# One attention and feed-forward kernel: sign tiles cleared on VectorE, block additions as separate plan entries, later landing times in the planner, casts on ScalarE, and the seven-product first layer from unit 3 on

## The chip, the cores and the metric

The kernel runs on one core of one Trainium2 chip. The metric is the device time of one launch in microseconds (us). Engines are called PE (TensorE), DVE (VectorE), ACT (ScalarE), POOL (GpSimd) and SP (SyncE, which here only issues transfers).

## The reference

Windowed attention with 8 global and 96 local keys and a slope per head, followed by a two-layer feed-forward block with a leaky activation:

```
scores = q @ k.T / sqrt(64) - slope[h] * dist          # B=4, H=8, S=768, D=64, masked to the window
a      = exp(scores - max) / (sum + 1e-9)
x      = (a @ v) as 3072 tokens x 512
h      = x @ w_in                                      # 512 x 2048
g      = max(h, 0) + alpha * min(h, 0)
out    = g @ w_out                                     # 2048 x 512, float32
```

## The kernel before

The 3072 tokens are cut into 12 units (u = 0 to 11) of 256 tokens. For each unit and each of 8 heads, `attend` makes the scores on PE (tile `sp`), the row minimum with bias on DVE (L651, `pr`, `sm`), the exponential on ACT (L656), a high and a low float16 part of the probabilities (`ps`), a transposing transfer on SP (`vp`), and the product with v on PE (`av`). `xn` is the normalised result of a unit.

Then the feed-forward block. All float32 operands are split in a high part (a cast, ACT or DVE) and a low part (the remainder, DVE, helper `rest`, L363 or L364), and every product is three float16 matmuls: high*high, high*low, low*high. The weights come as float64; `split_w` rebuilds a float32 from its two words (16 blocks f, tiles `wf`, `whl`). For blocks f from 6 on it uses two sign tiles `sg0`, `sg1` that `clear_signs` sets to zero once, on POOL.

The first layer has two forms. For u below `US` = 4, `ff_in2` computes `h` plainly: 16 blocks of 12 matmuls of 256 columns each (L894), `g` with one ACT scaling and one DVE step (L903), and its two halves `gg`. For u from 4 on, `ff_in4` computes four blocks f at once by a seven-product scheme on 2 x 2 blocks: 4 times 7 products of 12 matmuls of 128 columns in a unit (L827, banks `hx`, `hy`, `hz`), with sums of weight blocks `sw` (`combine_w`, eight of them, from `ws`) and sums of token blocks `t12`, `t34` (`x_combine`) in place of some operands, and with joins (L838, L855) and the activation (L863) on DVE in the tile `hs`, split as `ghl`. `ff_out` is the second layer, the same in both forms: 16 x 2 x 3 matmuls of 512 columns in a unit (L925).

The order of all work is made in the kernel itself. Every step is entered with a key (its due place), an engine and a cost (`op`, `copy`, `mul`, `rest`); `Plan.order` runs a list of events with these costs, with delays between engines (`LAG`), with the number of buffers of each tag, and picks on each engine the ready entry with the lowest key. Some entries have two possible engines: a first and another that takes it when the first has a long queue (`behind`, `FLEX`). The instructions are then issued in that order; each engine works strictly in order. A new cost or delay therefore moves many instructions by a few places. In the planner an SP entry is a transfer that is taken to land `LAG["SP"]` after its transfer time.

Of the kernel before, what the change touches and what calls it, by code (L numbers as in the profile page):

```python
# [136 lines left out]
class Plan:  # L137
# [7 lines left out]
    LAG = {"PE": 220, "DVE": 130, "ACT": 200, "POOL": 160, "SP": 1100}  # L145
# [27 lines left out]
    def order(self):  # L173
# [34 lines left out]
        while events:  # L208
# [11 lines left out]
            for e in engines:  # L220
# [73 lines left out]
LEAD1 = 22  # L294
# [10 lines left out]
XENG = ('DVE', 'DVE', 'POOL', 'ACT')  # L305
# [4 lines left out]
US = 4  # L310
QU = 4
SIGN = 6
# [12 lines left out]
def fast(tc, cn, a):  # L325
    nc = tc.nc
    ctx = ExitStack()
    with ctx:
# [184 lines left out]
        def combine_w(j, key):  # L513
# [4 lines left out]
            for i, x in enumerate((one_, two_)):  # L518
                cols = slice(512 * i, 512 * i + 512)
                on = lambda e, x=x, cols=cols: e.tensor_tensor(  # L520
                    out=r.t[:, cols], in0=x.t[:, 0, :512], in1=x.t[:, 1, :512], op=ALU.add)
                op("DVE", key, c_dve(512), lambda on=on: on(v), r=[(x, 0), (x, 2)], w=[(r, i)])

            def combine():
                q = [r.t[:, 256 * i : 256 * i + 256] for i in range(4)]
                v.tensor_tensor(out=q[3], in0=q[2], in1=q[3], op=ALU.add)
                v.tensor_tensor(out=q[2], in0=q[0], in1=q[2], op=ALU.subtract)
                v.tensor_tensor(out=q[0], in0=q[3], in1=q[0], op=ALU.subtract)
                v.tensor_tensor(out=q[1], in0=q[1], in1=q[0], op=ALU.subtract)
# [49 lines left out]
        def attend(u, h, key):  # L579
# [10 lines left out]
            if u > 1 and h % 2 == 0:  # L590
# [572 lines left out]
```

## Time and profile before

| what | value |
|---|---|
| median of 3 runs | 608.58 us (606.15 to 612.18) |
| the profiled execution | 606.35 us, its span 604.6 us |
| granted TensorE clock, mean | 0.996 of 2.4 GHz |
| busy: PE, DVE, ACT, POOL | 586.3, 502.8, 420.8, 3.9 us |
| first and last plain product (`h`) of units 2 and 3 | 140.4 to 185.7 us, 185.7 to 236 us |
| last matmul of the second layer | 595.9 us |

A busy PE means that matmuls are in flight; matmuls overlap, so that the price of one is read from the distance of the starts. The same holds for DVE, where a row's duration runs some 0.07 us into the next row's.

### The profile page before, as it was taken

To read this page: it belongs to the slowest core of one execution; us is meant where nothing else is said; L and a number is where in the kernel's file an instruction comes from. 1 tells how busy PE (TensorE), PEld (TensorE's weight loads), DVE (VectorE), ACT (ScalarE), POOL (GpSimd) and SP (SyncE) were. 2 spreads that over 40 slices of the span, in tenths; PEclk is the share of its full clock that TensorE was granted. 3 is DMA by queue.
4 is the path that set the end of the run, shared out by engine and by line. 5 is a ranking of instruction groups with operands and counts; after the bars stand their busy time and mean duration, and the time that the engine had idled before them with its cause. 6 is when DMAs were issued, how large, how long until landed. Compare 5 with 4: busy or idle time off the path is not lost.

```text
span 604.6 us, 15888 instructions
## 1 busy us (share of the span) xinstructions
PE 586.3 (97%) x6215; PEld 414.8 (69%) x6215; DVE 502.8 (83%) x1345; ACT 420.8 (70%) x1109; POOL 3.9 (1%) x13
## 2 busy tenths in 40 slices
PE   7999999999899999999999999999999999999994
PEld 6877666666566666877777777767777777777762
DVE  7999999999899979898799789788798788664441
ACT  5988999897747757778588688677586676552421
POOL 2000000000000000000000000000000000000000
PEclk9999999999999999999999999999999999999998
DMA  8996344355844436556649647539648625312001
GB/s 313 413 382 233 114 116 113 80 116 150 144 93 126 122 97 145 136 113 136 141 94 150 151 94 146 144 77 149 114 110 169 143 63 111 85 37 27 36 1 41
DMA packets 133795, 78.98 MB, mean 131 GB/s; under 512 B 114896, under 2 KB 116688, under 8 KB 133712
## 3 DMA queue, kind: packets, MB, share of 16 engines
q1 hardware_dynamic: 132992, 76.71, 51.6%
q10 hardware_dynamic: 720, 1.18, 0.6%
q8 instruction: 50, 0.82, 0.6%
q14 instruction: 33, 0.27, 0.1%
HBM read 43.79 MB, written 6.29 MB: 83 GB/s over the span
## 4 chain that ended last, share of the span: by engine, by line
PE 78%; DVE 16%; ACT 2%; issue 1%; DMA 1%; DVEq 0%; ACTq 0%
PE o L925 35%; PE hx L827 14%; PE h L894 8%; PE hy L827 7%; PE av L709 4%; PE hz L827 3%; PE sp L628 3%; PE sp L635 2%; DVE pr L651 2%; DVE ws L520 1%; DVE g L903 1%; DVE sw L363 1%; ACT pr L656 1%; DVE ps L364 1%; DVE gg L363 1%
## 5 line engine op out<-in xcount | busy, mean ns | idle before, releaser
L925 PE MATMUL o<-whl,ghl 128*128 128x512 f16 (+1 forms) x771 | 193.8, 379 | 0.0
L827 PEld LDWEIGHTS <-sw 128*128 128x128 f16 x1536 | 93.4, 98 | 21.1 <-issue 0.4
L925 PEld LDWEIGHTS <-ghl 128*128 128x128 f16 x771 | 66.9, 98 | 55.5 <-issue 5.1
L656 ACT ACTIVATE pr<-pr,sm 128x256 f32<-128x256 f32 (+1 forms) x192 | 92.4, 483 | 13.0 <-DVE sm L651 12.9
L894 PE MATMUL h<-xt,whl 128*128 128x256 f16 x768 | 92.3, 273 | 3.5 <-ACT g L344 2.2
L925 PE MATMUL o<-whl,gg 128*128 128x512 f16 x384 | 92.1, 379 | 1.8 <-DVE gg L363 1.7
L894 PEld LDWEIGHTS <-whl 128*128 128x128 f16 x768 | 73.7, 98 | 21.9 <-issue 7.7
L827 PEld LDWEIGHTS <-whl 128*128 128x128 f16 x1152 | 71.0, 98 | 18.9 <-issue 0.2
L651 DVE CUSTOM_DVE_ANT_0 pr<-sp,D 128x256 f32<-128x256 f32 (+1 forms) x192 | 69.8, 395 | 13.1 <-PE sp L628 12.0
L835 ACT ACTIVATE g<-hx 128x256 f32<-128x256 f32 x96 | 36.4, 380 | 60.4 <-PE hx L827 60.2
L863 DVE SCALAR_TENSOR_TENSOR hs<-hs,alpha 128x256 f32<-128x256 f32 x128 | 58.4, 479 | 18.0 <-ACT hs L835 17.1
L925 PEld LDWEIGHTS <-gg 128*128 128x128 f16 x384 | 35.6, 98 | 40.8 <-DVE gg L363 5.8
L364 DVE SCALAR_TENSOR_TENSOR ps<-pr,ps 128x512 f16<-128x512 f32 (+1 forms) x80 | 51.3, 643 | 7.6 <-ACT ps L344 7.4
L363 DVE TENSOR_TENSOR ghl<-hs,ghl 128x512 f16<-128x512 f32 x64 | 42.0, 685 | 2.2 <-ACT ghl L870 2.1
L870 ACT CAST ghl<-hs 128x512 f16<-128x512 f32 x64 | 36.8, 611 | 2.4 <-DVE hs L863 2.4
L344 ACT ACTIVATE ps<-pr 128x512 f16<-128x512 f32 (+1 forms) x60 | 36.1, 601 | 0.9
L656 ACT ACTIVATION_READ_ACCUMULATOR pr<-pr,sm 128x1 f32 x192 | 36.6, 191 | 0.0
L344 ACT ACTIVATE g<-h,ak 128x256 f32<-128x256 f32 x60 | 27.6, 462 | 9.8 <-PE h L894 9.7
L709 PEld LDWEIGHTS <-vp 128*128 128x128 f16 x888 | 30.5, 98 | 3.6
L835 ACT ACTIVATE hs<-hx 128x256 f32<-128x256 f32 x32 | 12.1, 379 | 29.1 <-PE hx L827 29.0
L709 PE MATMUL av<-vp 128*128 128x64 f16 x888 | 32.4, 193 | 0.0
L344 ACT ACTIVATE qs<-qk 128x672 f16<-128x672 f32 (+1 forms) x32 | 23.5, 733 | 12.2 <-PE sp L628 8.5
(137 smaller groups left out, 874.0 us busy)
## 6 DMA issues: line engine op xcount, KB each, us to landing
w<-in_w_dram SPq DMA_DIRECT2D x32, 512.0 KB, 8.3
qk<-in_qk_dram SPq DMA_DIRECT2D x28, 336.0 KB, 3.8
v<-in_vw_dram SPq DMA_DIRECT2D x28, 256.0 KB, 3.6
out_dram<-os SPq DMA_DIRECT2D x19, 256.0 KB, 3.5
qk<-in_qk_dram SPq DMA_DIRECT2D x12, 272.0 KB, 3.1
v<-in_vw_dram SPq DMA_DIRECT2D x12, 192.0 KB, 3.1
first<-in_first_dram SPq DMA_DIRECT2D x4, 464.0 KB, 4.7
first<-in_first_dram SPq DMA_DIRECT2D x4, 336.0 KB, 9.1
```

What stands on the lines that cost most here:

```text
L344: lambda: nc.scalar.mul(out=out(), in_=src(), mul=by.t if tile_ else by)),
L363: return e.tensor_tensor(out=out(), in0=src(), in1=hi(), op=ALU.subtract)
L364: return e.scalar_tensor_tensor(out=out(), in0=src(), scalar=val(), in1=hi(), op0=ALU.mult, op1=ALU.subtract)
L651: op("DVE", key, c_dve(n) + 10, lambda qb=qb, n=n, dc=dc, pc=pc: v.tensor_tensor_reduce(out=pr.t[:, pc : pc + n], in0=sp.t[:, pc : pc + n] ...
L656: op("ACT", key + 1, c_act(n, ptr=1) + 93, lambda qb=qb, n=n, pc=pc: nc.scalar.activation(out=pr.t[:, pc : pc + n], in_=pr.t[:, pc : pc + ...
L709: nc.tensor.matmul(out, lhsT=p_[:, 128 * j : 128 * j + 128], rhs=v_[:, 64 * j : 64 * j + 64], start=m == 0, stop=m == len(ps) - 1)
L827: nc.tensor.matmul(bank.t[:, 128 * q : 128 * q + 128], lhsT=wt(q, wi, c), rhs=xp(xi, c), start=begin and q == n == 0, stop=n == 5, skip_gr ...
L835: op("ACT", k, c_act(UT, True), lambda: nc.scalar.mul(out=out(), in_=two(bank), mul=KG), r=[bank], w=w, spare=SPARE if u < NU - 1 else 0)
L863: op("DVE", ks[4 + 2 * i], c_dve(UT, ptr=True), lambda n=n: v.scalar_tensor_tensor(out=hs.t[:, n, :], in0=hs.t[:, n, :], scalar=alpha[:, 4 ...
L870: op("ACT", ks[6], c_act(512), lambda q=q, cols=cols: nc.scalar.copy(out=ghl.t[:, 0, cols], in_=flat(q)), r=src, w=[(ghl, q)])
L894: nc.tensor.matmul(hp.t[:, cols], lhsT=w.t[:, wi, wc], rhs=x.t[:, NC * xi + c, :], start=n == 0, stop=n == 3 * NC - 1)
L925: nc.tensor.matmul(o.t[:, cols], lhsT=g_()[:, tok], rhs=w.t[:, wi, 512 + cols.start : 512 + cols.stop], start=f == 0 and n == 0, stop=f == ...
```

## The change

- `clear_signs` moves from POOL to DVE and is entered ahead of all other work; the tiles are set as 672 words of 32 bits each.
- The four additions of `combine_w` and of `x_combine`, each one plan entry before, become four entries with their own dependences, and `inverse` becomes `total` and `inverse`. The planner now takes 125 (before 60) between dependent DVE entries (`OWN`).
- Landings: `LAG["SP"]` 1100 becomes 2100, loads of q, k and v get 1500 more (`LOADS`), and a store on ACT's queue holds its buffer 2500 longer (`LANDS`).
- The v cast of units 2 and 3 has ACT as its first engine, as has the cast of the token block of unit 2 (`XENG`).
- `US` 4 becomes 3: unit 3 takes `x_combine` and `ff_in4`. `LEAD1` 22 becomes 24 (attention of unit 1 is due 2 earlier). The output tile of unit 1 uses the tag `pt`.

```diff
-    LAG = {"PE": 220, "DVE": 130, "ACT": 200, "POOL": 160, "SP": 1100}
+    LAG = {"PE": 220, "DVE": 130, "ACT": 200, "POOL": 160, "SP": 2100}
...
-                heapq.heappush(events, (end + self.LAG[e], i, "free"))
+                heapq.heappush(events, (end + self.LAG[e] + LANDS * (self.way[i].__name__ == "on_act"), i, "free"))
...
-                        at[j][x] = max(at[j][x], end + ((0 if e == "PE" else 60) if own else self.LAG[e] + self.spare[i]))
+                        at[j][x] = max(at[j][x], end + (OWN.get(e, 60) if own else self.LAG[e] + self.spare[i]))
...
-LEAD1 = 22
+LEAD1 = 24
...
-XENG = ('DVE', 'DVE', 'POOL', 'ACT')
+XENG = ('ACT', 'DVE', 'POOL', 'ACT')
...
-US = 4
+US = 3
 QU = 4
+LOADS = 1500
+LANDS = 2500
+OWN = {'PE': 0, 'DVE': 125}
...
         def clear_signs(key):
             for i in range(2):
                 x = buf("qs", f"sg{i}", [P, 1344], F16)
-                op("POOL", key, 1500, lambda x=x: nc.gpsimd.memset(x.t, 0.0), w=[x])
+                op("DVE", key, 700, lambda x=x: v.memset(x.t, 0.0), w=[x])
...
-            def combine():
-                q = [r.t[:, 256 * i : 256 * i + 256] for i in range(4)]
-                v.tensor_tensor(out=q[3], in0=q[2], in1=q[3], op=ALU.add)
-                v.tensor_tensor(out=q[2], in0=q[0], in1=q[2], op=ALU.subtract)
-                v.tensor_tensor(out=q[0], in0=q[3], in1=q[0], op=ALU.subtract)
-                v.tensor_tensor(out=q[1], in0=q[1], in1=q[0], op=ALU.subtract)
-
-            op("DVE", key, 4 * c_dve(256), combine, r=[], w=[r])
+            q = lambda i: r.t[:, 256 * i : 256 * i + 256]
+            for to, x, y, how in ((3, 2, 3, ALU.add), (2, 0, 2, ALU.subtract), (0, 3, 0, ALU.subtract), (1, 1, 0, ALU.subtract)):
+                op("DVE", key, c_dve(256), lambda to=to, x=x, y=y, how=how: v.tensor_tensor(
+                    out=q(to), in0=q(x), in1=q(y), op=how), r=[(r, x if y == to else y)] if to in (x, y) else [(r, x), (r, y)], w=[(r, to)])
...
-                    out=x.t[:, : 256 + nk], in_=a["qk"][u - 2, h // 2, :, : 256 + nk]), w=[x])
+                    out=x.t[:, : 256 + nk], in_=a["qk"][u - 2, h // 2, :, : 256 + nk]), w=[x], spare=LOADS)
...
-                mul(kp + 3, lambda: vhi()[:, :nv], vv, XS, [rv], [rvh], "ACT" if u >= US else "DVE", nv)
+                mul(kp + 3, lambda: vhi()[:, :nv], vv, XS, [rv], [rvh], "ACT", nv)
...
-                op("DVE", key + 3, 280, inverse, r=[(sm, (x, 2 + y)) for x in range(G) for y in range(2)], w=[(sm, "inverse")])
+                op("DVE", key + 3, 80, total, r=[(sm, (x, 2 + y)) for x in range(G) for y in range(2)], w=[(sm, "total")])
+                op("DVE", key + 3, 120, inverse, r=[(sm, "total")], w=[(sm, "inverse")])
...
-            op("DVE", key + 0.1, 4 * c_dve(256), combine, r=[x], w=[t12, t34])
+            combine(lambda: half(t12, 0), lambda: q(2), lambda: q(0), [x], [(t12, 0)])
+            combine(lambda: half(t34, 0), lambda: q(3), lambda: q(2), [x], [(t34, 0)])
+            combine(lambda: half(t12, 1), lambda: q(3), lambda: half(t12, 0), [x, (t12, 0)], [(t12, 1)])
+            combine(lambda: half(t34, 1), lambda: q(1), lambda: half(t12, 1), [x, (t12, 1)], [(t34, 1)])
...
-                s = buf("stage", f"os{u}_{t}", [P, 512]) if f == NF - 1 else None
+                s = buf("pt" if u == 1 else "stage", f"os{u}_{t}", [P, 512]) if f == NF - 1 else None
...
-        jobs = [(-99, clear_signs, ()), (-100, build_bias, ()), (-100, warm, ()), (slot(NU - 1, 6), check, ())]
+        jobs = [(-101, clear_signs, ()), (-100, build_bias, ()), (-100, warm, ()), (slot(NU - 1, 6), check, ())]
```

What the planner makes of it at three places. First, the start of the program on DVE (`ones`, `nf`, `tt`, `n2` are small constants, `ni` holds the two window sizes, `far` begins the bias). Before:

```order
L1111 MEMSET ones_63 128x128
L1124 CAST nf_68<-ni_66 128x4
L1126 SCALAR_TENSOR_TENSOR tt_70<-nf_68 128x2
L1127 SCALAR_TENSOR_TENSOR n2_69<-tt_70,nf_68 128x2
L405 TENSOR_SCALAR far_184<-rel_156,n2_69 128x256
```

With the change:

```order
L1115 MEMSET ones_63 128x128
L468 MEMSET sg0_156 128x672
L468 MEMSET sg1_182 128x672
L1128 CAST nf_68<-ni_66 128x4
L1130 SCALAR_TENSOR_TENSOR tt_70<-nf_68 128x2
L1131 SCALAR_TENSOR_TENSOR n2_69<-tt_70,nf_68 128x2
```

The two clears stand ahead of `nf` on DVE; on POOL they stood last, behind the making of `rel` and `gcol`.

Second, DVE in unit 3, where the first half of the activations (`gg3_0` before, `ghl3_0` now) is made for PE. Before:

```order
L903 SCALAR_TENSOR_TENSOR g3_0_2664<-h3_0_2635,g3_0_2664 128x512
L345 TENSOR_SCALAR g3_1_2780<-h3_1_2746,ak_153 128x256
L353 CAST sw6_2735<-ws6_2680 128x512
L364 SCALAR_TENSOR_TENSOR ps4_4_2778<-pr4_4_2719,ps4_4_2778 128x512
L363 TENSOR_TENSOR gg3_0_2783<-g3_0_2664,gg3_0_2783 128x512
```

With the change:

```order
L529 TENSOR_TENSOR ws5_2751<-ws5_2751 128x256
L865 SCALAR_TENSOR_TENSOR hs3_0_2749<-hs3_0_2749,alpha_65 128x256
L529 TENSOR_TENSOR ws5_2751<-ws5_2751 128x256
L865 SCALAR_TENSOR_TENSOR hs3_0_2749<-hs3_0_2749,alpha_65 128x256
L857 TENSOR_TENSOR hs3_0_2749<-g3_0_1_2782 128x2x128
L366 TENSOR_TENSOR sw5_2830<-ws5_2751,sw5_2830 128x512 x2
L650 ISA pr4_6_2927,sm4_4_2689<-sp4_6_2848,D6_216 128x256
L650 ISA sm4_4_2689 128x1
L865 SCALAR_TENSOR_TENSOR hs3_0_2749<-hs3_0_2749,alpha_65 128x256
```

In place of one activation step and one remainder there are joins, four activation steps and two remainders (`ghl3_0`, a few rows on), and the weight sums `ws5`, `sw5`, single entries now, stand between them.

Third, SP around the loads of q and k for unit 4. Before:

```order
L593 DMA qk4_0_2056<-in_qk_dram 128x672
L695 DMA_TRANSPOSE vp3_4_1934<-ps3_4_2092 128x6x128
L593 DMA qk4_2_2152<-in_qk_dram 128x672
L695 DMA_TRANSPOSE vp3_5_1951<-ps3_5_2111 128x6x128
L596 DMA v4_2_2185<-in_vw_dram 128x512
```

With the change:

```order
L592 DMA qk4_0_2086<-in_qk_dram 128x672
L697 DMA_TRANSPOSE vp3_4_1937<-ps3_4_2111 128x6x128
L697 DMA_TRANSPOSE vp3_5_1941<-ps3_5_2152 128x6x128
L592 DMA qk4_2_2185<-in_qk_dram 128x672
L595 DMA v4_2_2194<-in_vw_dram 128x512
```

The load of `qk4_2` has moved behind a second transposing transfer.

## Rows read from the trace of the kernel before

**Rows 1.** The page, busy tenths of PE and DVE in 40 slices of the span.

```profile
PE   7999999999899999999999999999999999999994
DVE  7999999999899979898799789788798788664441
```

**Rows 2.** Busy time of each engine by stretch, columns named in the first line.

```profile
core 0: us, PE busy (x) PEld busy (x) DVE busy (x) ACT busy (x) POOL busy (x), PEclk, DMA share, GB/s
...
195.00:210.00 15.00, 13.89 (x126) 9.63 (x125) 14.86 (x41) 11.94 (x33) 0.00 (x0) 1.00 0.41 105
210.00:225.00 15.00, 15.00 (x147) 10.09 (x146) 10.69 (x25) 7.58 (x20) 0.00 (x0) 1.00 0.47 120
225.00:240.00 15.00, 15.00 (x146) 10.18 (x145) 13.71 (x38) 11.17 (x29) 0.00 (x0) 1.00 0.54 122
240.00:255.00 15.00, 14.88 (x222) 11.72 (x220) 13.08 (x43) 13.33 (x41) 0.00 (x0) 1.00 0.49 140
```

**Rows 3.** Timeline, the start: start us, duration us, engine, line, operation, idle before.

```profile
2.11 2.37 POOL L465 MEMSET sg<- 128x1344 f16 x2
0.83 0.17 DVE L1111 MEMSET ones<- 128x128 f32 x1 [0.83 <-PEq L1153]
2.40 2.11 DVE L1124 CAST nf<-ni 128x4 f32<-128x4 int32 x1 [1.40 <-DMA ni<-in_n_dram]
...
8.50 0.28 DVE L651 CUSTOM_DVE_ANT_0 pr<-sp,D 128x128 f32<-128x128 f32 x1
```

**Rows 4.** What PE waited for: us in total, times, longest.

```profile
PE tp L676 <- ACT pr L656: 2.3, 2, 2.2
PE h L894 <- ACT g L344: 2.2, 2, 1.1
PE o L925 <- DVE gg L363: 1.7, 1, 1.7
```

**Rows 5.** Timeline around 156 us on SP, ACT and DVE.

```profile
151.25 2.13 SPq L593 DMA_DIRECT2D qk<-in_qk_dram  x1
156.28 0.77 ACT L344 ACTIVATE qs<-qk 128x672 f16<-128x672 f32 x1 [3.70 <-DMA qk<-in_qk_dram]
157.08 0.86 DVE L364 SCALAR_TENSOR_TENSOR qs<-qk,qs 128x672 f16<-128x672 f32 x1 [1.49 <-ACT qs L344]
```

**Rows 6.** Chain that ended last, and PE's timeline: start, duration, what, count.

```profile
52.44 2.62 PE h L894 x24
55.06 1.29 PE o L925 x6
214.60 0.76 PE sp L628 x12
255.46 1.34 PE hx L827 x24
...
211.78 0.86 PE L709 MATMUL av<-vp 128*128 128x64 f16 x24
212.48 0.81 PE L925 MATMUL o<-whl,gg 128*128 128x512 f16 x3
```

**Rows 7.** DVE's timeline at a weight sum and at an activation of unit 4.

```profile
140.49 0.41 DVE L526 TENSOR_TENSOR ws<-ws 128x256 f32<-128x256 f32 x1
140.94 0.43 DVE L527 TENSOR_TENSOR ws<-ws 128x256 f32<-128x256 f32 x1
...
141.86 0.43 DVE L529 TENSOR_TENSOR ws<-ws 128x256 f32<-128x256 f32 x1
142.20 0.68 DVE L520 TENSOR_TENSOR ws<-whl 128x512 f32<-128x512 f16 x1
142.80 0.75 DVE L353 CAST sw<-ws 128x512 f16<-128x512 f32 x2
...
249.09 0.48 DVE L863 SCALAR_TENSOR_TENSOR hs<-hs,alpha 128x256 f32<-128x256 f32 x1
249.49 0.42 DVE L651 CUSTOM_DVE_ANT_0 pr<-sp,D 128x256 f32<-128x256 f32 x1
```

More of the change, by code (lines that the diff above doesn't have):

```diff
@@ L593, in attend @@
                 op("SP", kp - 4, c_dma(P * 4 * (256 + nk)), lambda: nc.sync.dma_start(
-                    out=x.t[:, : 256 + nk], in_=a["qk"][u - 2, h // 2, :, : 256 + nk]), w=[x])
+                    out=x.t[:, : 256 + nk], in_=a["qk"][u - 2, h // 2, :, : 256 + nk]), w=[x], spare=LOADS)
                 y = buf("v", "v" + uh, [P, 512])
                 op("SP", kp - 4 + (1 if late else 0), c_dma(P * 8 * nv), lambda: nc.sync.dma_start(
-                    out=y.t[:, : 2 * nv], in_=a["vw"][u - 2, :, h * nv : (h + 2) * nv]), w=[y])
+                    out=y.t[:, : 2 * nv], in_=a["vw"][u - 2, :, h * nv : (h + 2) * nv]), w=[y], spare=LOADS)
                 for i in range(2):
@@ L660, in attend, with total, inverse @@
                     r=[(sm, (n_, qb))], w=[(pr, qb), (sm, (n_, 2 + qb))])
-            def inverse():
+            def total():
                 v.tensor_scalar(out=sm.t[:, 4 * G : 6 * G], in0=sm.t[:, 2 * G : 4 * G], scalar1=1e-9,
                                 scalar2=1.0 / XS if plain and u >= XDMA else 1.0 if plain else PSC, op0=ALU.add, op1=ALU.mult)
+            def inverse():
                 v.reciprocal(out=sm.t[:, 6 * G :], in_=sm.t[:, 4 * G : 6 * G])
             if n_ == G - 1:
-                op("DVE", key + 3, 280, inverse, r=[(sm, (x, 2 + y)) for x in range(G) for y in range(2)], w=[(sm, "inverse")])
+                op("DVE", key + 3, 80, total, r=[(sm, (x, 2 + y)) for x in range(G) for y in range(2)], w=[(sm, "total")])
+                op("DVE", key + 3, 120, inverse, r=[(sm, "total")], w=[(sm, "inverse")])
             if plain:
@@ L766, in x_combine, with combine @@
             half = lambda t, i: t.t[:, 256 * i : 256 * i + 256]
-            def combine():
-                v.tensor_tensor(out=half(t12, 0), in0=q(2), in1=q(0), op=ALU.subtract)
-                v.tensor_tensor(out=half(t12, 1), in0=q(3), in1=half(t12, 0), op=ALU.subtract)
-                v.tensor_tensor(out=half(t34, 0), in0=q(3), in1=q(2), op=ALU.subtract)
-                v.tensor_tensor(out=half(t34, 1), in0=q(1), in1=half(t12, 1), op=ALU.subtract)
+            def combine(out, x, y, r, w):
+                op("DVE", key + 0.1, c_dve(256), lambda: v.tensor_tensor(out=out(), in0=x(), in1=y(), op=ALU.subtract), r=r, w=w)
             a_ = buf("xt", f"xt{u}", [P, 16, P], F16)
@@ L941, in ff_out, with on_act @@
                     on = nc.scalar if u < 2 or parts_ > 1 and part == 0 else nc.sync
-                    store = lambda on=on, s=s, rows=rows, cols=cols: on.dma_start(
-                        out=a["out"][rows : rows + 128, cols], in_=s.t[:, cols])
+                    def on_act(on=on, s=s, rows=rows, cols=cols):
+                        on.dma_start(out=a["out"][rows : rows + 128, cols], in_=s.t[:, cols])
                     if on is nc.sync:
-                        op("SP", key, c_dma(P * 4 * n_), store, r=[z])
+                        op("SP", key, c_dma(P * 4 * n_), lambda store=on_act: store(), r=[z])
                     else:
-                        op("ACT", key, 100, store, r=[z])
+                        op("ACT", key, 350, on_act, r=[z])
         def warm(key):
```

10 lines of the change are left out of this document (5 added, 5 removed).

## The prediction

> **What bounds the kernel now.** I read the page's busy tenths first: PE stands at 9 in every slice but the first and the last, and DVE stands at 9 until about slice 14, then at 7 to 9 [rows 1]. So PE is the engine whose work makes the time, and in the first 210 us DVE feeds it without slack. The busy times by stretch show where that changes: DVE works 14.86 of 15 us up to 210 us, then 10.69, 13.71 and 13.08, so 4.3 + 1.3 + 1.9 = 7.5 us of DVE lie idle between 210 and 255 us while PE is full [rows 2]. A shorter time can come from three things only: less PE work, less waiting of PE, an earlier start. PE's own list of waits is short: 2.3 us at the first transposes (`tp`), 2.2 us in two waits of `h` for ACT's scaling `g` (near 31 and 208 us), 1.7 us of `o` for `gg` (at 162 us) [rows 4]. The sum below is made against the profiled execution, 606.35 us; the median of the three runs, 608.58, lies 0.4% above it.
>
> **Term 1, the products of unit 3: minus 2.2 us.** A plain unit has 16 x 12 = 192 matmuls of 256 columns; 24 of them take 2.62 us, so 0.109 each and 20.9 us in all. A seven-product unit has 4 x 7 x 12 = 336 matmuls of 128 columns; 24 take 1.34 us, so 0.056 each and 18.8 us [rows 6]. The second layer is the same in both (6 matmuls of 512 columns in 1.29 us). PE is full on both sides of this stage, so the 2.2 us count in full unless PE waits for something new.
>
> The Trainium skill, "TensorE: Matmul & The Clock Gate", section "Back-to-back issue gap", speaks against this: with a weight load ahead of each matmul it gives some 81 ns as the sustained spacing at 128 columns. By it, unit 3 would take 336 x 0.081 = 27.2 us, an estimate from that page. This case's trace differs, 56 ns a matmul with a load each, and the row is what the sum uses.
>
> **Term 2, the start: minus 1.8 us.** `nf` is a cast of 4 words and takes 2.11 us on DVE, from 2.40 to 4.51. POOL's two clears of the sign tiles run from 2.11 to 4.48, and the cast ends with them; the first `pr` follows at 8.50 and PE's first transposes wait for that chain [rows 3, 4]. With the clears off POOL the cast can start when `ni` has landed, at 2.40. But the clears now stand ahead of it on DVE, from 1.00 on (end of `ones`). A clear of 672 words is not in the trace. From below, it costs no less than the `ones` row, 0.17 us for 128 words; from above, 672/128 x 0.17 = 0.89. Two take 0.34 to 1.78 and end between 1.34 and 2.78 us, so `nf` starts at 2.40 to 2.78 and, at the 0.17 of a small DVE row, ends at 2.57 to 2.95 instead of 4.51. That is 1.6 to 1.9 us; I take 1.8, since the scaled row is the nearer one. If the cast were slow by itself the term is 0. The following 8 us are a chain of DVE, ACT and PE, whose first link on PE is the wait of 2.2 us, long enough to give back the whole [rows 4].
>
> The Trainium skill, "SBUF — State Buffer", section "SBUF: two separate sides", says why: a DVE cast in a two-port mode and a GpSimd instruction take one shared pair of ports as an exclusive lock, and the later one blocks fully. A DVE memset has no SBUF input, so by that page the clears run beside POOL's `iota` work at no loss; were they to queue with it the gain would be about 1 us smaller. The rows agree as far as the cast goes; no row here shows the memset.
>
> **Term 3, waits that go: minus 3.0 us.** At 151.25 us SP holds the load `qk` for a buffer for 2.13 us; it lands at 156.28, ACT has waited 3.70 us in front of it, DVE 1.49 behind ACT [rows 5], and 5 us later PE waits 1.7 us for `gg` [rows 4]. With the change the load is issued even later, behind a second transposing transfer. But its buffer comes free with the last scores of unit 3 in either order, and its reader, the split `qs4_2`, now stands on DVE behind the `gg` steps of blocks 4 to 7 of unit 2, so nothing stands still in front of it. DVE has also 1.5 to 2 us less to do up to those `gg` steps (next part). I count 1.4 of the 1.7 as gone. The wait near 208 us was one of plain `h` for `g` in unit 3 and disappears with that form: 1.1. In the first 50 us the order of the two first `h` blocks and the attention of unit 1 changes so that the wait at 31 us is covered, and up to the token block of unit 1, which PE waits for next, DVE has about 0.5 us less to do: 0.5. Together 3.0, between 0 (each wait comes back elsewhere) and 3.9 (all of it and nothing new).
>
> **Term 4, DVE in unit 3: plus 2.0 us.** Prices by distance of starts [rows 7]: 0.60 for 512 columns with two inputs (142.20 to 142.80), 0.45 for an addition that follows the one it depends on (140.49 to 140.94), 0.34 for one that does not (141.86 to 142.20), 0.40 for an activation step L863 (249.09 to 249.49).
> Added: in each of four `ff_in4` blocks three joins (0.34) and four activation steps (0.40), 2.6 us, 10.5 in the unit, for eight steps L903 of 0.60 taken away, 4.8; and four block additions and the larger split of the tokens (one more remainder of 0.60, one of 0.34), 2.3. Plus 8.0.
> Removed: the additions of the eight weight sums, 3 x 0.45 + 0.34 each, become 4 x 0.34 where others stand between them: 8 x 0.35 = 2.8. From DVE to ACT go, by the order, 7 `vp` casts (0.2 each, the smaller part of the 0.34 class), 4 `sw` casts (0.75 for two, less the overlap) and one `xs` cast: 3.0. ACT works 7.6 to 13.3 of 15 us in these stretches [rows 2] and takes them in its gaps; without that cover each would cost about 0.5. Minus 5.8.
> The net of 2.2 us fits in the 7.5 idle us. What counts is the place: the removals lie ahead of unit 3, the additions inside it. From `gg2_5` to the first `ghl3_2` the order of the changed kernel has on DVE 35 rows at 0.60, 52 of the 0.34 class, 12 at 0.40 and 14 others (three at 0.77, three at 0.45, the rest casts and small ones), together 49.7 us. On PE, between the same two tiles, stand 300 matmuls of 128 columns, 84 of 512, 36 of 256, 60 score and 96 value matmuls; at 0.056, 0.215, 0.109, 0.76/12 and (212.48 - 211.78)/24 us [rows 6] that is 45.4 us, some 46 with the small gaps. DVE comes into this stretch about 1.5 us ahead of where it was, since so much of the removals lies before it. So PE waits about 49.7 - 1.5 - 46 = 2.2 us less a few tenths for `total` and `inverse`, which no longer follow each other directly: 2.0. The ends are 0 (DVE has all removals ahead of it) and 3.7 (the lead is lost). After that DVE finds the idle 7.5 us and catches up before unit 4 needs `ghl4_0`; from unit 6 on the orders of before and after are the same piece by piece, and so is the tail.
>
> **Sum.** 606.35 - 2.2 - 1.8 - 3.0 + 2.0 = 601.35, forecast 601.3 us.
>
> **Rivals.**
> - *DVE is covered in unit 3.* The 7.5 idle us speak for it, that they lie behind 210 us and not before speaks against. Terms 1 and 2 whole, the named waits gone (3.9), no new one: 606.35 - 2.2 - 1.9 - 3.9 = 598.3.
> - *The start gives nothing and unit 3 waits.* `nf` is slow by itself, or the load stream, on which the first weights depend, takes the place of the chain; DVE arrives in unit 3 without its lead. For it speaks that DVE is full until 210 us, so any slip stays: 606.35 - 2.2 - 3.0 + 3.7 = 604.9.
> - *Slower: DVE becomes the bound of unit 3 whole.* If the 8.0 us added there are paid in full, because the 5.8 removed lie where DVE has no one waiting, the time is 606.35 - 2.2 + 8.0 = 612.2. It decides from the point where DVE's lag in unit 3 is over 2.2 + 1.8 + 3.0 = 7 us. Against it: DVE leaves unit 2 with a lead, and the count above gives 2.
> - *Slower by the weight loads.* If 128-column matmuls took 81 ns where sums and blocks alternate, unit 3 would cost 6.3 us more instead of 2.2 less: 601.3 + 8.5 = 609.8. Units 4 to 11 run this very form at 56 ns [rows 6], so it gets little. (The figure is that of the Trainium skill's "Back-to-back issue gap"; from rows alone this rival would end at the forecast.)
>
> **How the numbers follow.** Chances: forecast 0.45 (its own range 599.3 to 603.3), covered 0.20, start gives nothing 0.25, DVE bound 0.08, weight loads 0.02. The range that leaves out no more than 2 in 10 reaches from a little under the covered case to a little over the third: 597.0 to 606.0. About 1% is what a measurement of this kernel tells from no change, 6.1 us; that border lies at 600.3 by the profiled execution and at 602.5 by the median, in the middle of the forecast's own range. So half of the forecast and the covered case give faster: 0.20 + 0.25 = 0.45; the other half and the third case give same: 0.20 + 0.25 = 0.45; slower 0.10.
>
> **What would show it.** Term 2 is right if `nf` lasts some 0.2 us and the first `pr` comes near 6.7 us; it is wrong if the row still lasts 2 us. Term 1 is right if the `hx`, `hy`, `hz` groups of unit 3 show 24 in 1.34 us. Term 3: no wait of PE for `gg` near 160 us, no wait of ACT for `qk`. Term 4: PE's list of waits names `ghl` (DVE L366) between 190 and 225 us with 1 to 4 us. The forecast is wrong at its root if PE waits in places that it does not wait at now, above all for transfers whose issue has been moved on SP, or if DVE shows idle time in the first 150 us.

## The result, and the profile after

With the change the kernel takes 601.12 us (median of 6 runs, 600.50 to 602.34), without it 606.96 (median of 6): ratio 0.989, with a 95% interval from 0.986 to 0.993. The profiled execution took 600.72 us, its span 598.9, against 606.35 and 604.6 before. The forecast was 601.3.

| what | before | after |
|---|---|---|
| profiled execution, us | 606.35 | 600.72 |
| PE's first transposes (`tp` of unit 0) start | 9.37 | 8.20 |
| PE's last `h` of unit 1 ends | 133.52 | 132.43 |
| PE's last matmul of the second layer ends | 595.86 | 590.83 |
| from the last `h` of unit 1 to the last matmul | 462.34 | 458.40 |
| from the last matmul to the end of the span | 8.70 | 8.07 |
| busy: PE, DVE, ACT | 586.3, 502.8, 420.8 | 584.8, 502.9, 426.5 |

Of the 5.6 us between the two profiled executions 1.1 lie ahead of unit 2, 3.9 behind that, and 0.6 behind the last matmul, where the change moves nothing. PE is 5.03 us ahead at the last `hx` of unit 4 and exactly as much at its last matmul: all is settled in the first 280 us. The row "from the last `h` of unit 1 to the last matmul" is called **the stretch** from here on.

The start on DVE and PE after the change, from the timeline (start us, duration us, engine, line, operation, idle time before), answers [rows 3]:

```profile
1.08 1.33 DVE L468 MEMSET sg<- 128x672 uint32 x2
2.40 0.17 DVE L1128 CAST nf<-ni 128x4 f32<-128x4 int32 x1
...
7.31 0.29 DVE L650 CUSTOM_DVE_ANT_0 pr<-sp,D 128x128 f32<-128x128 f32 x1 [0.66 <-PE sp L634]
...
5.63 0.94 PEld L634 LDWEIGHTS sp<-first 64*128 64x128 f32 x8 [0.22 <-DMA first<-in_first_dram]
6.76 0.96 PEld L634 LDWEIGHTS sp<-first 64*128 64x128 f32 x8 [0.19 <-DMA first<-in_first_dram]
```

The cast takes 0.17 us instead of 2.11, the chain on DVE is 1.94 us earlier; but now DVE waits 0.66 us for the first scores, and these wait for their loads. The first `pr` moves from 8.50 to 7.31 only.

PE's list of waits after the change (in total, times, longest), answers [rows 4]:

```profile
PE o L927 <- DVE ghl L366: 1.6, 2, 1.4
PE tp L678 <- ACT pt L682: 1.2, 2, 0.7
PE h L896 <- DVE g L905: 0.5, 1, 0.5
PE h L896 <- DMA xt<-xs: 0.3, 1, 0.3
PE o L927 <- DVE gg L366: 0.3, 1, 0.3
```

The waits of `tp` for `pr` (2.2 us, 0.2 left), of `h` for ACT's `g` (2.2) and the 1.7 us for `gg` (0.3 left) are gone; one of 1.4 us for `ghl` is new, and two for `pt` in the first 40 us.

Busy time by stretch after the change, with the columns of [rows 2]:

```profile
195.00:210.00 15.00, 14.74 (x201) 11.11 (x199) 15.00 (x40) 11.27 (x31) 0.00 (x0) 1.00 0.34 57
210.00:225.00 15.00, 13.61 (x166) 9.37 (x164) 15.00 (x40) 12.42 (x33) 0.00 (x0) 1.00 0.39 95
225.00:240.00 15.00, 15.00 (x206) 11.11 (x203) 15.00 (x45) 12.28 (x38) 0.00 (x0) 1.00 0.92 177
240.00:255.00 15.00, 15.00 (x194) 10.77 (x191) 12.90 (x40) 10.86 (x31) 0.00 (x0) 1.00 0.58 152
```

DVE (the third pair) now works 15.00 of 15 us up to 240 us: the 5.6 idle us that it had between 210 and 240 us before are filled, and it has idle time again only behind 240. The new wait, in the chain that ended last (start, duration, what):

```profile
219.86 0.39 DVE hs L865
220.25 1.01 DVE t L771 x3
221.26 0.60 DVE xs L366
221.86 0.34 DVE t L771
222.19 0.34 DVE xs L366
222.53 0.61 DVE ghl L366
223.14 0.05 issue
223.19 1.04 PE o L927 x4
```

The last activation step of `ghl3_2` ends near 220.25. Six rows of the token block of unit 4 (`t`, `xs`), 2.3 us in all, follow on DVE before the remainder that PE waits for.

### The profile page after: what moved, and what is told of

The parts are those of the page before. It is cut to its first block, busy times and chain, and to the rows that moved or that the text cites. A ratio compares the mean times of both kernels' runs of the same rounds, so it can differ in the third digit from the quotient of the medians.

```text
span 598.9 us, 16204 instructions
## 1 busy us (share of the span) xinstructions
PE 584.8 (98%) x6359; PEld 416.1 (69%) x6359; DVE 502.9 (84%) x1363; ACT 426.5 (71%) x1125; POOL 1.6 (0%) x11
## 4 chain that ended last, share of the span: by engine, by line
PE 72%; DVE 18%; ACT 6%; issue 2%; DMA 1%; POOL 0%; POOLq 0%
PE o L927 33%; PE hx L829 15%; PE hy L829 7%; PE av L711 4%; PE hz L829 4%; PE h L896 4%; PE sp L627 3%; DVE pr L650 2%; DVE whl L367 2%; DVE wf L506 1%; DVE ws L529 1%; ACT pr L655 1%; DVE gg L366 1%; PE sp L634 1%; DVE g L905 1%
## 5 line engine op out<-in xcount | busy, mean ns | idle before, releaser
L927 PE MATMUL o<-whl,ghl 128*128 128x512 f16 x867 | 218.3, 379 | 1.6 <-DVE ghl L366 1.6
L829 PEld LDWEIGHTS <-sw 128*128 128x128 f16 x1728 | 104.7, 98 | 22.6 <-issue 0.2
L927 PEld LDWEIGHTS <-ghl 128*128 128x128 f16 x867 | 75.1, 98 | 64.3 <-issue 5.3
L829 PEld LDWEIGHTS <-whl 128*128 128x128 f16 x1296 | 79.6, 98 | 20.7 <-issue 0.6
L865 DVE SCALAR_TENSOR_TENSOR hs<-hs,alpha 128x256 f32<-128x256 f32 x144 | 65.8, 479 | 19.9 <-ACT hs L837 18.9
L896 PE MATMUL h<-xt,whl 128*128 128x256 f16 x576 | 68.9, 273 | 1.0 <-DVE g L905 0.5
L927 PE MATMUL o<-whl,gg 128*128 128x512 f16 x288 | 67.8, 379 | 0.3 <-DVE gg L366 0.3
L896 PEld LDWEIGHTS <-whl 128*128 128x128 f16 x576 | 55.2, 98 | 14.6 <-issue 4.1
L927 PEld LDWEIGHTS <-gg 128*128 128x128 f16 x288 | 27.1, 98 | 30.2 <-issue 2.4
L367 DVE SCALAR_TENSOR_TENSOR vp<-v,vp 128x256 f16<-128x256 f32 (+1 forms) x80 | 31.1, 395 | 0.0
L829 PE MATMUL hz<-xt,whl 128*128 128x128 f16 x432 | 30.0, 219 | 0.0
```

The costliest lines, as they stand in the source:

```text
L367: return e.scalar_tensor_tensor(out=out(), in0=src(), scalar=val(), in1=hi(), op0=ALU.mult, op1=ALU.subtract)
L829: nc.tensor.matmul(bank.t[:, 128 * q : 128 * q + 128], lhsT=wt(q, wi, c), rhs=xp(xi, c), start=begin and q == n == 0, stop=n == 5, skip_gr ...
L865: op("DVE", ks[4 + 2 * i], c_dve(UT, ptr=True), lambda n=n: v.scalar_tensor_tensor(out=hs.t[:, n, :], in0=hs.t[:, n, :], scalar=alpha[:, 4 ...
L896: nc.tensor.matmul(hp.t[:, cols], lhsT=w.t[:, wi, wc], rhs=x.t[:, NC * xi + c, :], start=n == 0, stop=n == 3 * NC - 1)
L927: nc.tensor.matmul(o.t[:, cols], lhsT=g_()[:, tok], rhs=w.t[:, wi, 512 + cols.start : 512 + cols.stop], start=f == 0 and n == 0, stop=f == ...
```

## The experiments

All twelve are parts of the change, put into the kernel before or taken out of the changed one, small edits of the changed kernel, or the changed kernel again. The ratio is to the kernel before on the same chip. Places and the stretch are those of one profiled execution each; where one program was profiled twice, or the edit lies outside the stretch, the stretch repeats within 0.15 us (458.40, 458.48 and 458.34; 457.03 and 457.04; 462.34 and 462.41), much closer than the medians do. The stretch is not the whole time, though: with what lies ahead of it and behind it a program can move by another 2 us (e5 below). Three small parts of the change have no run of their own: `LEAD1`, the split of `inverse`, and the split of the additions of `x_combine`.

| kernel | `tp` | last `h`, unit 1 | last matmul | stretch | median | ratio to before, interval |
|---|---|---|---|---|---|---|
| before | 9.37 | 133.52 | 595.86 | 462.34 | 606.4 to 607.0 | |
| changed | 8.20 | 132.43 | 590.83 | 458.40 | 601.12 | 0.989 (0.986 to 0.993) |
| e8 changed, again | 8.70 | 132.56 | 591.04 | 458.48 | 601.77 | 0.992 (0.990 to 0.994) |
| e1 clears on POOL | 9.38 | 135.17 | 593.51 | 458.34 | 604.15 | 0.995 (0.993 to 0.997) |
| e2 tokens later | 8.07 | 132.82 | 589.85 | 457.03 | 600.21 | 0.987 (0.984 to 0.991) |
| e3 plain unit 3 | 7.68 | 131.96 | 590.69 | 458.73 | 601.36 | 0.990 (0.986 to 0.994) |
| e4 casts on DVE | 7.45 | 131.68 | 590.51 | 458.83 | 599.73 | 0.988 (0.984 to 0.992) |
| e5 old landings | 8.53 | 131.72 | 593.96 | 462.24 | 602.47 | 0.993 (0.991 to 0.994) |
| e6 additions joined | 8.41 | 132.33 | 594.21 | 461.88 | 605.23 | 0.998 (0.996 to 0.999) |
| e7 before, clears on DVE | 7.44 | 132.99 | 595.40 | 462.41 | 605.29 | 0.997 (0.995 to 0.999) |
| e9 before, single additions | 9.37 | 135.61 | 597.43 | 461.82 | 609.41 | 1.005 (1.003 to 1.008) |
| e10 before, form in unit 3 | 9.38 | 133.53 | 602.91 | 469.38 | 616.87 | 1.017 (1.014 to 1.020) |
| e12 before, new landings | 9.38 | 135.08 | 595.97 | 460.89 | 606.63 | 1.000 (0.996 to 1.003) |
| e11 tokens later, alpha by ACT | 8.07 | 132.32 | 589.36 | 457.04 | 599.77 | 0.988 (0.986 to 0.990) |

### The start: e1 and e7

```diff
 e1, the changed kernel:
-                op("DVE", key, 700, lambda x=x: v.memset(x.t, 0.0), w=[x])
+                op("POOL", key, 1500, lambda x=x: nc.gpsimd.memset(x.t, 0.0), w=[x])
 (e7, the kernel before: the same lines the other way round)
```

> The changed kernel with the two clears of the sign tiles back on POOL; every other row of every engine stands as in the changed kernel. Theory (the start is worth what PE's first transposes moved, 9.37 to 8.20 us): the cast nf lasts 2.1 us again, the first transposes come near 9.4, and the 1.2 us go through to the end: 601.1 + 1.2 = 602.3 us. Rival (the loads of the first weights set the first product h, whatever the start does): the first h stands where it stands now, near 26.6, and the time stays at 601.1. Second rival (the whole length of the cast counts): 601.1 + 1.9 = 603.0.

> The kernel before with the two clears on DVE and nothing else. Theory (the start is a matter of the cast nf alone): nf lasts 0.2 us, PE's first transposes come 1.2 to 1.9 us earlier than 9.37 us, and PE's last h of unit 1 as much earlier than 133.52 us; the stretch behind it stays 462.34 us; 607.0 - 1.2 to 1.9 = 605.1 to 605.8 us. Rival (the loads give the pace of the first 20 us): the first transposes come earlier, but xp of unit 0 stays near 22.9 us: 607.0.

Timeline of e1 on DVE and PE, and a row of its busy times (TensorE's granted clock, as a share of full speed, is the 0.50 behind POOL's pair):

```profile
2.42 2.09 DVE L1128 CAST nf<-ni 128x4 f32<-128x4 int32 x1 [1.42 <-DMA ni<-in_n_dram]
...
7.25 0.93 PE L634 MATMUL sp<-first 64*128 64x128 f32 x8 [1.20 <-DMA first<-in_first_dram]
9.38 0.33 PE L678 MATMUL tp<-ident,pr 128*128 128x128 f32 x1 [1.20 <-ACT pr L655]
10.24 0.93 PE L634 MATMUL sp<-first 64*128 64x128 f32 x8
11.75 1.66 PE L634 MATMUL sp<-first 64*128 64x128 f32 x8
...
12.00:14.00 2.00, 2.00 (x11) 1.35 (x12) 0.50 (x4) 1.21 (x5) 0.00 (x0) 0.50 1.02 416
```

The cast lasts 2.09 us again and `tp` stands at 9.38: that part is as the theory had it, and e7 shows it from the other side:

```profile
2.40 0.17 DVE L1124 CAST nf<-ni 128x4 f32<-128x4 int32 x1
...
7.44 0.33 PE L676 MATMUL tp<-ident,pr 128*128 128x128 f32 x1 [0.36 <-ACT pr L656]
9.69 0.93 PE L635 MATMUL sp<-first 64*128 64x128 f32 x8 [1.31 <-DMA first<-in_first_dram]
```

Here `tp` comes the whole 1.93 us earlier, and then PE waits 1.31 us for the next of the first loads; at the last `h` of unit 1 only 0.53 are left. The median, 605.29, is 1.4 us below that of the kernel before on the same chip (606.72). So the cast was the bound, and behind it stand the loads, whose landing differs from profile to profile: in those with the clears on DVE, `tp` starts anywhere from 7.44 to 8.70.

The median of e1, 604.15, lies above its expectation of 602.3. In its profile the last `h` of unit 1 is 2.74 us later than in the changed kernel. Of these, 1.2 are the later `tp`; the rest comes from TensorE's clock, which stands at 0.50 of full speed, 1.2 GHz, from 12 to 14 us, after PE had waited twice for 1.20 us: eight score matmuls take 1.66 us instead of 0.93. The same is seen in e12 (clears on POOL too), and not in the profiles of the kernel before, of e9 or of e10, with waits of about that length. That is a second thing that a late start can cost, some 1.5 us in these two profiles.

The mean granted clocks of all executions show that this is no rare case. Of the 12 executions of e1, seven have a mean under 0.994 (0.991 to 0.993, at 603.67 to 606.31 us); of the 12 of the changed kernel (its own and those of e8) none has. These programs differ in the place of the clears alone. So by medians that place is worth 2.4 to 3.0 us in the changed kernel (604.15 against 601.77 and 601.12, on different chips), more than the 1.1 us between the first two profiles. Where the clock was low in executions without a profile is not known.

### The new wait: e2

```diff
-                jobs.append((begin(u) + 2 * H + 3, x_combine, (u,)))
+                jobs.append((begin(u) + 2 * H + 3 + (1.5 if u == 4 else 0), x_combine, (u,)))
```

> The changed kernel with the token block of unit 4 due 1.5 places later, so that the remainders of ghl3_2 come ahead of six of its rows (t12, t34, xs) on DVE. Theory (PE's wait of 1.4 us for ghl near 221 us is a matter of place, six rows of some 2.4 us that nobody waits for yet stand in front): the wait goes, PE comes to unit 4 some 1.4 us earlier: 601.1 - 1.4 = 599.7 us. Rival (DVE's sum of work is what PE waits for): the wait comes back at the next ghl or at hx of unit 4 with the same length: 601.1. Second rival (the tokens of unit 4 are late then): PE waits for xt near 230 us, 601.1 or more.

The stretch is 457.03 us, 1.37 shorter; the median is 600.21. The chain of e2 at the place, and PE's row behind it:

```profile
220.39 0.60 DVE ps L367
221.00 0.60 DVE ghl L366
...
221.94 0.60 DVE ghl L366
...
221.36 3.40 PE L927 MATMUL o<-whl,ghl 128*128 128x512 f16 x15
```

The remainders of `ghl3_2` start at 220.93 and 221.87 instead of 222.45 and 223.65, and PE runs its 15 matmuls of `o` without a gap. DVE has the same rows to do as before. So the wait was one of place: what PE needs stood behind what nobody needed yet. Of the second rival, 0.2 us at `hy` near 231 us is all that shows. The median moved 0.9, not 1.4, which the spread of the starts (0.4 us later here than in the first profile of the changed kernel) and of the ends covers.

### The form: e3 and e10

```diff
 e3, the changed kernel:        e10, the kernel before:
-US = 3                         -US = 4
+US = 4                         +US = 3
```

(In e10 the v casts of unit 3 were kept on DVE.)

> The changed kernel with the plain first layer in unit 3, as before the change. Theory (the form saves 2.1 us of PE work and pays it in part with 1.6 us of waits for ghl, in place of about 1.1 us of waits of h for g): 601.1 + 2.1 - 1.6 + 1.1 = 602.7 us, PE waits for g or gg in unit 3 and not for ghl. Rival (the waits of unit 3 are there in either form): 601.1 + 2.1 = 603.2. Second rival (the form gives nothing net, DVE bounds unit 3 in either): 601.1 or less, as DVE has 8 us less to do.

> The kernel before with the seven-product form in unit 3 and nothing else: sums as one entry, old landings, old casts. Same stretch, 462.34 us before. Theory (without the lead DVE pays the 8.0 us that the form adds in unit 3, beyond the 2.1 us that PE saves and some of the idle DVE time behind 210 us): 464 to 468 us in the stretch, 608 to 612 us in all, PE waits for ghl in several places between 195 and 240 us. Rival (the form is worth its 2.1 us by itself): 460.2 us in the stretch, 604.9 in all.

e3: the stretch is 458.73, so **the form is worth 0.33 us** in the changed kernel, by one profile of each, and the median, 601.36, does not differ. Neither the theory (1.6 more) nor the first rival (2.1 more) came; the second one is nearest. PE's waits in e3:

```profile
PE h L896 <- DVE g L905: 0.6, 1, 0.6
PE h L896 <- ACT g L347: 0.3, 1, 0.3
```

The first of these lies near 50 us. In unit 3 the plain form has one wait of 0.3 us left of the 1.1 us that it had near 208 us before the change. So it does not take the form to remove it, as the prediction said: in e12 (below), the kernel before with the new landings, unit 3 is plain too, and `h` does not wait for `g` there. The theory's "plus 1.1" is what failed.

e10: the stretch is 469.38, **7.04 us more** than before, beyond the theory's upper end (5.7 more), and the median is 10.5 us above that of the kernel before (616.87 against 606.39). Three of PE's waits, the timeline of PE and ACT, and a row of busy times:

```profile
PE h L894 <- ACT g L344: 3.6, 2, 2.5
PE o L925 <- ACT ghl L870: 1.1, 2, 0.7
PE o L925 <- DVE ghl L363: 0.9, 2, 0.4
...
143.15 0.60 ACT L936 ACTIVATE os<-o 128x512 f32<-128x512 f32 x1 [2.01 <-DMA out_dram<-os]
...
242.78 1.22 PE L827 MATMUL hy<-xt,sw 128*128 128x128 f16 x12 [2.88 <-ACT hs L835]
244.15 1.44 PE L827 MATMUL hx<-xt,sw 128*128 128x128 f16 x12 [0.15 <-ACT g L835]
245.38 1.36 PE L827 MATMUL hz<-xt,whl 128*128 128x128 f16 x12
...
241.80 0.66 ACT L344 ACTIVATE qs<-qk 128x544 f16<-128x544 f32 x1 [2.92 <-DMA qk<-in_qk_dram]
...
244.00:247.00 3.00, 2.85 (x26) 2.62 (x26) 2.97 (x8) 2.69 (x8) 0.00 (x0) 0.59 0.51 117
```

Waits for `ghl` in four places between 203 and 217 us are there, as expected, 2.0 us in all. Beside them stand three things that were not expected. In unit 2, at 145 us and ahead of the form, ACT stands 2.01 us in front of a store of `os` that is still under way, and PE's `h` waits 2.5 behind it. Near 240 us ACT stands 2.92 us in front of a load of qk, and PE waits 2.88 behind it. And then the clock is low (a mean of 0.59 from 244 to 247 us), so that three groups of twelve matmuls take 1.2 us instead of 0.67, together 1.64 us with the small wait taken off. Without this last part it is 5.4 us, inside the expected range, but the two waits behind transfers are larger than those for `ghl`, so that DVE's added work is not what most of it shows; from 240 to 255 us DVE is busy for 11.75 of 15 us. The granted clocks of the six executions reach from 0.976 to 0.994, which goes with a median further off than the stretch.

### What makes the form affordable: e4, e5, e6

```diff
 e4:
-XENG = ('ACT', 'DVE', 'POOL', 'ACT')
+XENG = ('DVE', 'DVE', 'POOL', 'ACT')
-                mul(kp + 3, lambda: vhi()[:, :nv], vv, XS, [rv], [rvh], "ACT", nv)
+                mul(kp + 3, lambda: vhi()[:, :nv], vv, XS, [rv], [rvh], "ACT" if u > 3 else "DVE", nv)
 e5:
-    LAG = {..., "SP": 2100}      LOADS = 1500      LANDS = 2500
+    LAG = {..., "SP": 1100}      LOADS = 0         LANDS = 0
 e6 (combine_w):
-            four entries op("DVE", key, c_dve(256), ...), each with its own reads and writes
+            one entry op("DVE", key, 4 * c_dve(256), combine, r=[], w=[(r, i) for i in range(4)])
```

> The changed kernel with the casts of v in units 2 and 3 and of the tokens of unit 2 back on DVE as first engine. Theory (DVE is full from 135 to 240 us, the casts are worth up to 3.0 us of it, and what is taken from DVE ahead of unit 3 is the lead with which it enters): PE's waits for ghl or gg between 150 and 225 us grow by 1.5 to 3.0 us: 602.6 to 604.1 us. Rival (some of these casts went to ACT in any case, and DVE has slack where they stand): 601.1.

> The changed kernel with the old landings in the planner (SP 1100, loads and stores without their additions). All numbers for the stretch from PE's last h of unit 1 to PE's last matmul, which was 462.34 us before and 458.40 us with the change. Theory (the new place of the load of qk and of its split is what took PE's wait of 1.7 us for gg near 162 us away): the load is issued early again, ACT waits for it over 2 us, PE waits for gg: 458.4 + 1.4 = 459.8 us in the stretch. Rival (DVE's lead took it away, wherever the load stands): 458.4 within 0.3 us. Second rival (the landings matter in more places): over 460.5.

> The changed kernel with the four additions of a weight sum again as one entry of the plan, each waiting for the one ahead of it, 0.45 us instead of 0.34. Same stretch, 458.40 us with the change. Theory (eight sums give DVE 2.8 us between 135 and 216 us, where it is full, and this is the lead with which it enters unit 3): PE's waits for gg and ghl grow by 1 to 2.8 us: 459.4 to 461.2 us. Rival (the lead is there without it, or is lost elsewhere): 458.4 within 0.3 us.

e4: the stretch grows by 0.43 us only, so the casts are worth little: the rival was nearer. Its median is 1.4 us *below* that of the changed kernel. By the profiled executions that comes from the start (0.75, there already at `tp`) and from behind the last matmul (1.08), where the written rows of both kernels are the same. Whether the program itself brings that about is not known; it stays open.

e5 (the plan's cost of a store, 350, and the tag of unit 1's output stay as changed): the stretch is 462.24, 3.84 more: nearly the whole gain in the stretch, as the second rival had it (more places than one). But PE's wait for `gg` near 162 us did not come back, and so the theory fell in its place, if not in its kind. Rows of SP, ACT and PE:

```profile
230.86 0.35 SPq L592 DMA_DIRECT2D qk<-in_qk_dram  x1
235.83 0.66 ACT L347 ACTIVATE qs<-qk 128x544 f16<-128x544 f32 x1 [2.85 <-DMA qk<-in_qk_dram]
237.33 0.83 PE L829 MATMUL hy<-xt4c,sw 128*128 128x128 f16 x12 [1.81 <-ACT g L837]
```

It is the picture of [rows 5], 80 us later and at another load: issued at 230.86, landed near 235.8, ACT in front of it for 2.85 us, PE behind ACT for 1.81. The wait for `ghl` grew as well, to 2.0 us at 223 us. ACT's or DVE's longest wait for a load or store under way (`qk`, `v`, `os`) is 3.7 us in the kernel before, 2.9 in e5, 2.9 in e10 and 2.0 in e9; with the new landings it is 0.4 or less (the changed kernel, e2, e3, e12).

The whole time does not show the 3.84 us. The median, 602.47 (601.61 to 602.97), lies only 0.7 us above that of the changed kernel on the same chip (e8, 601.77). In the two profiles e5 is 0.8 us ahead at the last `h` of unit 1, and its time behind the last matmul is 1.7 us shorter (6.9 against 8.7). No run shows whether the old landings bring these two about. So 3.84 us is what the landings are worth in the stretch; what they are worth in all is 0.7 us by these medians.

e6: the stretch is 461.88, 3.48 more, above the theory's 1.0 to 2.8. PE's waits, and the four additions of one sum on DVE:

```profile
PE o L930 <- DVE ghl L366: 1.5, 4, 0.4
PE o L930 <- ACT ghl L875: 1.1, 2, 0.7
PE o L930 <- DVE gg L366: 0.6, 1, 0.6
PE sp L630 <- DVE sm L653: 0.6, 1, 0.6
...
154.60 1.81 DVE L531 TENSOR_TENSOR ws<-ws 128x256 f32<-128x256 f32 x4
156.33 0.55 DVE L367 SCALAR_TENSOR_TENSOR ps<-pr,ps 128x384 f16<-128x384 f32 x1
```

Four dependent additions in a row hold DVE for 1.73 us, from 154.60 to the next row at 156.33; single ones with others between them take 4 x 0.34 = 1.36. For the seven sums inside the stretch that is 2.6 us. The rest of the 3.48 no run separates; the joined entry also makes the first half of each `sw` wait for all four additions. PE waits for DVE or ACT in all of unit 3, in pieces of 0.4 to 0.7 us, and 0.6 us for `gg` near 160 us is back. The median, 605.23, is 3.5 us above that of e8 on the same chip, as the stretch has it.

### Each part alone: e9 and e12

```diff
 e9 (the kernel before): combine_w with four single entries, as in the changed kernel; 125 between dependent entries of DVE
 e12 (the kernel before): SP 2100, LOADS 1500, LANDS 2500, stores by on_act at a cost of 350, os1 in the tag pt
```

> The kernel before with the four additions of a weight sum as single entries (and 125 between dependent entries of DVE), nothing else: plain unit 3, old landings, old casts. Stretch from PE's last h of unit 1 to PE's last matmul, 462.34 us before. Theory (the eight sums are worth 2.8 us of a full DVE, and that lead is what takes PE's waits of 1.7 us at 162, 0.7 at 185 and 1.1 at 208 us away): 458.8 to 460.0 us in the stretch, 603.5 to 604.5 us in all. Rival (the waits go only when additions, landings and casts come together, as each one taken back alone gave back nearly all): 462.0 or more in the stretch, 606.7 in all.

> The kernel before with the new landings alone (SP 2100, loads of q, k and v 1500 more, stores on ACT's queue 2500 more, the output tile of unit 1 in another tag). Theory, formed after the runs with the landings and the additions taken back (the landings keep ACT from standing in front of a load that is still under way, 2.9 to 3.7 us in each profile with the old landings, none over 0.4 us in those with the new): ACT has no wait of over 1 us for qk between 130 and 250 us, and in the stretch from PE's last h of unit 1 to its last matmul PE loses its wait of 1.7 us for gg: 462.34 - 1.7 = 460.6 us. Rival (DVE, without its lead, is late by about as much): ACT's wait goes, but the stretch stays over 461.8 us. Second rival (the landings alone bring the whole 3.9 us): 458.5 us.

e9: the theory fell, and the rival is nearer. The stretch is 0.52 us shorter, not 2.3 to 3.5, and what lies ahead of it is 2.1 longer: 609.41 us. No weight sum stands there before 125.8 us, so it is the new price of dependent entries that moves the first units. PE waits for `gg` in three places instead of one (the two waits for `xt` are those near 50 us, ahead of the stretch):

```profile
PE o L921 <- DVE gg L363: 1.4, 3, 0.7
PE h L890 <- ACT xt L344: 1.2, 1, 1.2
PE h L890 <- DVE xt L364: 1.0, 1, 1.0
```

e12: ACT has no wait for qk any more, and the stretch is 460.89, 1.45 less than before, where 1.7 less was expected. What is left is DVE's lateness, in four pieces:

```profile
PE o L927 <- DVE gg L365: 1.3, 4, 0.4
```

In the profile the 1.45 us are lost again ahead of the stretch, 1.56 us, with the same low clock near 12 us as in e1. The median does not move either (606.63 against 607.04, ratio 1.000), and the fastest executions of both are alike (605.01 and 605.05), so that no time shows the landings to gain anything alone.

So the parts do not add up one by one. In the stretch, alone against the kernel before: landings -1.45, additions -0.52, clears 0.07, form +7.04. Taken away from the changed kernel: landings +3.84, additions +3.48, casts +0.43, form +0.33. One rival is left open: every one of these edits also makes the planner order many rows anew, and e2 shows that six rows in another place can be worth 1.4 us. No run changes a cost or a delay in a way that should not matter, so how much of each figure is the part itself, and how much is the place at which rows happened to fall, is not shown.

### The changed kernel again, and a faster one: e8 and e11

> The changed kernel once more. Theory (what differs between executions of one program lies in the landing of the first loads and of the last store, and nowhere between them): the stretch from PE's last h of unit 1 to PE's last matmul is 458.40 us within 0.1, the first transposes come between 7.4 and 8.3 us, the end of the span 7 to 9.5 us behind the last matmul; the median is 601.1 within 0.7 us. Rival (the waits of PE in units 2 and 3 differ too from execution to execution): the stretch differs by 0.5 us or more.

The theory held: 458.48 in the stretch, `tp` at 8.70 (0.4 outside of its range), 8.7 us behind the last matmul, median 601.77.

```diff
 e11 = e2 and:
-    load_alpha=lambda: nc.sync.dma_start(out=alpha, in_=a["alpha"])
+    load_alpha=lambda: nc.scalar.dma_start(out=alpha, in_=a["alpha"])
```

> The changed kernel with the token block of unit 4 due 1.5 places later, and the small load of alpha issued by ACT, so that SP issues the second to fourth of the first loads 0.45 us earlier; every other row as in the kernel with the tokens later. Theory (PE's second pair of first scores waits for the second load, 0.2 to 1.0 us in the profiles so far): xp of unit 0 comes 0.2 to 0.5 us earlier, the stretch from PE's last h of unit 1 to its last matmul is 457.03 us: 599.7 us in all. Rival (the landing of these loads is set by the transfers and not by the issue): xp of unit 0 near 22.3 us, 600.2 in all.

The stretch is that of e2 to 0.01 us. `xp` of unit 0 starts at 21.98 us, 0.5 earlier than in e2 but inside the 21.36 to 22.50 of the other profiles with this start, so what the alpha load does stays open. At 599.77 us (599.08 to 600.10) it beats both kernels, by the place of the token block.

## Why the prediction came out right

**The total** is right (601.3 against 601.12), closer than its parts, and that is luck. By the profiles, the prediction gave 2.3 us to the time ahead of unit 2 (1.8 and 0.5), where 1.1 came, and 2.7 us to the stretch (2.2 + 2.5 - 2.0), where 3.9 came: two misses of 1.2 us that cancel. Some of the reasons are wrong where the size is not.

**Term 1 (minus 2.2).** Held. Twelve matmuls of `hx`, `hy` or `hz` in unit 3 take 0.67 us, as in units 4 to 11, 56 ns a matmul, and the stretch shows no other pace. The 81 ns of the Trainium skill, "TensorE: Matmul & The Clock Gate", section "Back-to-back issue gap", are not borne out here.

**Term 2 (minus 1.8).** The mechanism held and the size, in the first profile, did not: 1.2 us at `tp` and 1.1 at the last `h` of unit 1 (0.5 in e7, 1.0 in e8, up to 1.8 in the others). The clears cost 1.33 us, inside the estimate, and the cast 0.17. The step that failed is "long enough to give back the whole": it asked how long PE waited, and not what PE would wait for next, the landing of the first loads. That was named as a possibility only in the rival "the start gives nothing". On the other side, a late start can also bring the clock down (e1, e12), which no term had, and by medians the clears' place is worth 1.4 (e7) to 3.0 us (e1). (The traces agree with the exclusive lock of the Trainium skill, "SBUF — State Buffer", section "SBUF: two separate sides", as far as the cast goes: 2.09 us beside POOL's clears, 0.17 without them.)

**Term 3 (minus 3.0).** About right in size: in the stretch the kernel with the plain form (e3) gains 3.61 us with the same products on PE, against the 2.5 counted for the waits at 162 and 208 us (another, of 0.5 in PE's list at 185 us, went too); the 0.5 counted for the first 50 us did not come (PE is 1.17 us ahead at `tp` and 1.09 at the last `h` of unit 1: the wait at 31 us went, but two for `pt`, 1.2 us, came). The reasons were half right. With the new landings alone ACT no longer stands in front of the load, as said, and the wait at 162 us shrinks to pieces of 0.4 (e12); but with the old landings and the rest of the change (e5) it is gone too, so the load's place is one way to lose it and not the only one. The wait at 208 us was said to go with the plain form; e3 has the plain form and 0.3 us of it.

**Term 4 (plus 2.0).** The size held, the reason did not. PE's list has 1.6 us, where and on what it was forecast, and terms 1 and 4 together are -0.33 (e3) against the -0.2 predicted. But the working counted 49.7 us of DVE against 46 of PE, as if DVE's sum decided; e2 took 1.37 us of the wait away without taking a row from DVE. What decided was the place of six rows, which the sum doesn't hold, so the agreement in size is luck as well. And the lead of 1.5 us that it leans on is not a thing of the additions alone: in the stretch 3.48 us are lost without them (e6), and 3.84 without the landings (e5).

**The rival "DVE becomes the bound of unit 3 whole"** got 0.08 and 612.2 us, and that chance stood for the full package. The form without the rest (e10, 616.87 us) is slower still, but not by that rival's mechanism: waits of ACT for transfers and the low clock behind one of them are the larger part.

So the change is a gain at the start (1.1 us in the profiles, 1.4 to 3.0 by medians of e7 and e1), a form that pays for itself by 0.3 us, and 3.6 us of waits that go with landings, additions and casts planned anew. That they go because landings and additions are planned nearer to what they take fits e5, e6 and e12, but is not shown against any other new order. The prediction gave most of its gain to waits that go, and that is the part that came out.

## What to carry to other kernels

Where one engine is full, an edit that adds to it and an edit that relieves it have no price of their own: here the same form costs 7.0 us of the stretch alone, in an order that also runs into two transfers, and gains 0.3 in company, so that it has to be tried with the relief and without it. Look at the whole time beside the stretch: a part worth 3.8 us in the one was worth 0.7 in the other. When a wait is removed, ask what that engine waits for next; at the start of this program it was a load. And in a hand-made order look at the rows that stand directly in front of the one that is waited for: moving six rows that nobody needed yet was worth more (1.4 us) than a cheaper form of the products.

## What the runs showed of the hardware that was not expected

TensorE's clock fell to 0.50 in the middle of the program after one wait of 2.88 us (e10), and cost 1.6 us more than the wait itself; and it stood at 0.50 from 12 to 14 us in e1 and e12, behind PE's waits at the start (1.20 twice; 2.26 at `tp`), while in the profiles of the kernel before and of e9 waits of nearly that length (2.16 at `tp`; 1.49 and 0.69) left it at 1.00. A wait on PE can thus cost more than its length, and not each time.

In the profiled executions programs differ at their ends and hardly between them: the stretch of over 450 us repeats within 0.15 us, while the first transposes moved by 1.3 us (7.44 to 8.70) among the kernels with the clears on DVE, where they wait for the first loads, and the time behind the last matmul lay between 6.9 and 9.4 us. Executions with a mean clock of 0.98, at 612 us and more, are on record for kernels with the clears on POOL, and none of them has a profile.
